# Attention q in 64-row tiles, eight heads at a time, with the vector work and the transposes in a hand-made order

## The chip, the cores and the metric

One core of a Trainium2 chip. The metric is the device time of one execution in microseconds (us). Where runs are compared they are of the same state (fast), and their intervals are at 95%.

## The reference, cut to what matters

One transformer block over 2048 tokens of width 576, everything in bf16: attention with 32 query heads on 16 cached K/V heads, a "mixer" with shifts by 1 and 2 tokens, and an MLP.

```python
x = A_x
xn = _layernorm(x)
q = (xn @ wq)                         # (2048, 576) @ (576, 4096): 32 heads of 128
k, v = the last 512 cached rows of each of 16 heads, each used by two query heads
o = softmax(q k^T * 128**-0.5) v
s = o @ wo                            # (2048, 4096) @ (4096, 576)
h = gelu(layernorm(xn) @ w1)          # mixer; its columns are shifted by +1, -1, +2, -2 tokens
x1 = xn + shifted(h) @ w2
g = silu(x1 + gelu(layernorm(x1) @ w3) @ w4)
return x + s * g
```

## The kernel before

The attention runs in 128 **units**: one head, one block of 512 queries. Four blocks of 32 units. PE, POOL and SP follow the program's order; DVE and ACT are ordered by a scheduler, in which `high_priority` moves an operation ahead. A unit is five q matmuls (576 rows padded to 5 x 128), four score matmuls, four exponentials on ACT, sixteen narrow P·V matmuls, a reciprocal and a multiplication on DVE for each half of them, and a transpose of the result by a DMA that SP issues:

```python
def stage_q(u):
    ...
    for kc in range(NDC):                                   # 5 chunks of 128 rows, the last half empty
        nc.tensor.matmul(psq[:, :], lhsT=w[:, kc, hh * Dh:(hh + 1) * Dh], rhs=xT_b[qb % 2][:, kc, :], ...)
    ... qT is copied by DVE in the first block, by ACT later ...

def stage_v(u, t0):
    ...                                                     # o_pool has 4 buffers
    with tc.high_priority(offset=HP):
        nc.vector.reciprocal(out=ri, in_=po[:, :, Dh])
        nc.vector.tensor_tensor(out=o[:, t0:t0 + 2, :], in0=po[:, :, 0:Dh], in1=ri..., op=ALU.mult)

def stage_t(u):
    o = o_t.pop(u)
    oT = oT_pool.tile([P, TB, P], BF16, name="oT")
    last_t[0] = nc.sync.dma_start(out=oT[:], in_=o[:]..., transpose=True)

for u in range(...):                                        # PE's order
    for i in range(4):
        stage_s(u, i)
        if i == 0:
            stage_q(u + 1)                                  # one q per unit
            for fn in fill.get(u, []): fn()                 # loads, layernorm, LN transposes
            continue
        if i < 3: stage_v(u - 1, 2 * (i - 1))
        ...                                                 # output projection and mixer matmuls in the gaps
    stage_t(u - 1)
```

All of the weights are loaded by POOL while the first block runs. Where in the program each load stands is set by a unit number.

```python
def load_wq(j, eng=None):                                   # four heads of wq: two requests
    eng.dma_start(out=w[:, 0:NF, :], in_=...)               # 512 KB
    eng.dma_start(out=w[0:DR, NF, :], in_=...)              # 64 KB
...
at(2, lambda: late(pT_t[2][0][0:1, 0:1], load_w1))          # late: a small POOL copy that waits for unit 2
at(10, gather_w1)
for i in range(8):
    at(4 + 3 * i, lambda i=i: late(pT_t[4 + 3 * i][0][0:1, 0:1], lambda: load_wo(i)))   # 576 KB each
at(4, lambda: load_k(2))
at(12, lambda: load_k(3))                                   # 512 KB
for g in range(4, Hkv, 2):
    at(2 * g - 8, lambda g=g: load_v(g // 2))               # two requests of 128 KB
for j in range(2, NB * 8):
    at(4 * (j - 1) - 1, lambda j=j: load_wq(j))
```

## Time and profile before

| | before |
|---|---|
| time | 855.94 us, median of 3 runs (852.17 to 856.51) |
| span of the profiled run | 847.5 us |
| PE busy | 98% of the span |

The lines that the prediction rests on stand in it. Beside them, the windows of the kernel before: the time before the first exponential is 12.9 us, then come the first block of attention, the second, and (the last line) everything after the attention. Columns: the stretch, its us, busy us and count of PE, PEld, DVE, ACT and POOL, the granted clock, the DMA share, GB/s.

```profile
12.90:116.00 103.10, 99.97 (x851) 62.75 (x867) 80.42 (x260) 75.75 (x134) 30.90 (x52) 1.00 0.85 182
116.00:249.80 133.80, 132.79 (x1104) 79.29 (x1122) 65.10 (x225) 92.27 (x172) 17.40 (x30) 1.00 0.45 96
521.50:847.50 326.00, 315.65 (x3609) 174.87 (x3617) 140.42 (x383) 103.02 (x174) 1.67 (x2) 1.00 0.29 79
```

One group of the page, the operation that frees a P·V bank and fills an o buffer:

```profile
L387 DVE TENSOR_TENSOR o<-po,ri_b 128x256 bf16<-128x256 f32 x256 | 107.9, 422 | 10.7 <-DMA oT<-o 4.3
```

Of DVE's idle time ahead of it 4.3 us were ended by a DMA: a transpose had not yet given its o buffer back.

### The profile page before, as it was taken

How to read it: one execution, taken by the hardware profiler on the slowest of the kernel's cores; microseconds unless marked ns; L12 is line 12 of the kernel's file. 1: busy time of each engine (PE TensorE's matmuls, PEld its weight loads, DVE VectorE, ACT ScalarE, POOL GpSimd, SP SyncE). 2: the span in 40 equal slices, each digit the busy share in tenths (PEclk: the TensorE clock that was granted, in tenths of full speed). 3: DMA queues.
4: the chain of work that ended last, by engine and by line, in shares of the span. 5: the costliest groups of instructions: out<-in, count | busy, mean ns of one | idle time of the engine just before them, and what ended most of it. 6: DMA issues, size and time to landing. Idle time of an engine off the chain costs nothing.

```text
span 847.5 us, 19375 instructions
## 1 busy us (share of the span) xinstructions
PE 826.8 (98%) x7896; PEld 485.0 (57%) x7980; DVE 427.7 (50%) x1351; ACT 460.9 (54%) x825; POOL 76.9 (9%) x134
## 2 busy tenths in 40 slices
PE   8999899999999999999999999999999999999996
PEld 5665555665564565565566565455555555555555
DVE  5778841267751166762154884052247537635324
ACT  5776763598793388784379874132333333334610
POOL 3441200310010111010001100000000000000000
PEclk9999999999999999999999999999999999999999
DMA  7996751473372174363048336992003301310101
GB/s 181 234 234 159 157 97 41 117 125 91 87 136 43 41 130 99 91 126 82 19 82 164 70 79 105 307 342 47 2 2 74 99 2 43 69 64 15 44 15 46
DMA packets 139983, 83.94 MB, mean 99 GB/s; under 512 B 106944, under 2 KB 133248, under 8 KB 139888
## 3 DMA queue, kind: packets, MB, share of 16 engines
q1 hardware_dynamic: 130048, 53.01, 30.6%
q0 software_dynamic: 8448, 28.15, 11.8%
q10 hardware_dynamic: 1392, 1.48, 0.5%
q8 instruction: 64, 1.05, 0.5%
q14 instruction: 31, 0.25, 0.1%
HBM read 49.17 MB, written 9.44 MB: 69 GB/s over the span
## 4 chain that ended last, share of the span: by engine, by line

## 5 line engine op out<-in xcount | busy, mean ns | idle before, releaser
L367 ACT ACTIVATE pT<-sc 128x512 bf16<-128x512 f32 x512 | 290.3, 596 | 103.5 <-PE sc L365 91.4
L365 PE MATMUL sc<-qT,kT 128*128 128x512 bf16 x493 | 175.1, 378 | 1.3 <-DVE qT L355 0.6
L382 PEld LDWEIGHTS <-pT 128*128 128x128 bf16 x2048 | 139.5, 98 | 52.9 <-DVE o L387 2.5
L382 PE MATMUL po<-v_sb,pT 128*128 128x129 bf16 x2048 | 161.4, 220 | 3.2 <-DVE o L387 2.0
L350 PE MATMUL psq<-xT_b,wq_b 128*128 128x512 bf16 x603 | 151.9, 379 | 2.5 <-DMA xT_b<-xn_b 0.4
L386 DVE RECIPROCAL ri_b<-po 128x2 f32<-128x2 f32 x256 | 43.0, 168 | 189.3 <-PE po L382 185.3
L731 PE MATMUL ph<-xT_b,w_s 64*128 64x512 bf16 x976 | 127.1, 376 | 2.3 <-DVE fence L721 2.1
L768 PE MATMUL pm<-w_s,h 64*128 64x512 bf16 x864 | 122.2, 377 | 0.9 <-DVE fence L721 0.9
L406 PE MATMUL pswo<-wo_sb,oT 128*128 128x512 bf16 x497 | 114.2, 379 | 0.8
L387 DVE TENSOR_TENSOR o<-po,ri_b 128x256 bf16<-128x256 f32 x256 | 107.9, 422 | 10.7 <-DMA oT<-o 4.3
L749 ACT ACTIVATE h<-ph 128x512 bf16<-128x512 f32 x67 | 39.4, 597 | 133.9 <-PE ph L731 133.9
L350 PEld LDWEIGHTS <-wq_b 128*128 128x128 bf16 x640 | 62.4, 98 | 74.4 <-issue 2.2
L768 PEld LDWEIGHTS <-h 64*128 64x128 bf16 x1728 | 70.8, 94 | 56.7 <-issue 1.6
L406 PEld LDWEIGHTS <-oT 128*128 128x128 bf16 x1024 | 64.9, 98 | 55.2
L768 PE MATMUL pr<-w_s,h 64*128 64x64 bf16 x864 | 90.2, 189 | 0.2 <-ACT h L749 0.2
L731 PEld LDWEIGHTS <-w_s 64*128 64x128 bf16 x1152 | 57.3, 94 | 51.0 <-issue 2.8
L357 ACT ACTIVATE qT<-psq 128x512 bf16<-128x512 f32 x96 | 57.4, 598 | 28.1 <-PE psq L350 26.7
L747 DVE COPY hx<-ph 128x512 f32<-128x512 f32 x55 | 38.0, 692 | 67.8 <-PE ph L731 67.8
L365 PEld LDWEIGHTS <-kT 128*128 128x128 bf16 x512 | 47.4, 97 | 28.4 <-DVE qT L355 1.2
L227 POOL DMA_DIRECT2D wq_b<-in_A_wq_dram x30 | 23.4, 780 | 314.4 <-PE psq L350 295.4
L721 DVE TENSOR_SCALAR fence<-ph,ph 1x1 f32<-1x1 f32 x61 | 12.6, 206 | 53.9 <-PE ph L731 53.4
L749 ACT ACTIVATE h<-hx 128x512 bf16<-128x512 f32 x55 | 34.6, 630 | 8.5 <-DVE hx L747 7.0
(114 smaller groups left out, 641.3 us busy)
## 6 DMA issues: line engine op xcount, KB each, us to landing
wq_b<-in_A_wq_dram POOLq DMA_DIRECT2D x30, 512.0 KB, 5.3
w_s<-in_B_w_dram SPq DMA_DIRECT2D x9, 576.0 KB, 7.0
wo_sb<-in_A_wo_dram POOLq DMA_DIRECT2D x8, 576.0 KB, 5.0
w_s<-in_B_w_dram SPq DMA_DIRECT2D x9, 512.0 KB, 7.9
x_dram<-x SPq DMA_DIRECT2D x4, 576.0 KB, 3.5
x<-x_dram SPq DMA_DIRECT2D x4, 576.0 KB, 5.1
s_b<-s_dram SPq DMA_DIRECT2D x4, 576.0 KB, 5.4
x_b<-in_A_x_dram SPq DMA_DIRECT2D x4, 576.0 KB, 6.6
```

What stands on the lines that cost most here:

```text
L350: nc.tensor.matmul(psq[:, :], lhsT=w[:, kc, hh * Dh:(hh + 1) * Dh], rhs=xT_b[qb % 2][:, kc, :], start=(kc == 0), stop=(kc == NDC - 1))
L357: nc.scalar.activation(out=qT[:, :], in_=psq[:, :], func=ACT.Copy)
L365: nc.tensor.matmul(sc[:, :], lhsT=kT[:, g, kc * P:(kc + 1) * P], rhs=qT_t[u][:, :], start=True, stop=True)
L367: nc.scalar.activation(out=pT[:, :], in_=sc[:, :], func=ACT.Exp, scale=SCALE)
L382: nc.tensor.matmul(po[:, j, :], lhsT=pTs[kc][:, tt * P:(tt + 1) * P], rhs=v_sb[:, g, kc, 0:Dh + 1], start=(kc == 0), stop=(kc == KCH - 1))
L386: nc.vector.reciprocal(out=ri, in_=po[:, :, Dh])
L387: nc.vector.tensor_tensor(out=o[:, t0:t0 + 2, :], in0=po[:, :, 0:Dh], in1=ri.unsqueeze(2).to_broadcast([P, 2, Dh]), op=ALU.mult)
L406: nc.tensor.matmul(ps, lhsT=oT_t[qb * Hq + h][:, tt, :], rhs=wo_sb[:, h, lo:hi], start=(h == 0), stop=(h == Hq - 1))
L731: nc.tensor.matmul(ps[i][:, :], lhsT=lhsT, rhs=xT[half, kc, :], start=first, stop=last, skip_group_check=True)
L747: nc.vector.tensor_copy(out=src[:, :], in_=ps[i][:, :])
L749: nc.scalar.activation(out=h3[:, :], in_=src[:, :], func=ACT.Gelu_apprx_tanh)
L768: nc.tensor.matmul(out, lhsT=h3_t[b, fc][half, tt * P:(tt + 1) * P], rhs=w4_s[fc // WS][half, fc % WS, lo:hi], start=key not in started, s ...
```

## The change

**Intent.** q for two heads takes nine slots in place of ten, by running the two 64-row halves of the PE array on different heads; eight heads at a time (four in the first block), so that the change of tiling is paid seldom. DVE and ACT join the engines that follow the program's order; their small work is handed out in pieces by a budget. LN transposes wait in a list and are issued between those of the attention outputs. The mixer's stages move later, and so do the loads of w1 (eleven units) and wo (five units); the wq loads of the first block move two units earlier.

The diff, cut to its core:

```diff
-        o_pool = pool("o_pool", 4)
+        o_pool = pool("o_pool", 5)
...
         def load_wq(j, eng=None):
-            eng.dma_start(out=w[0:DR, NF, :], in_=A_wq[NF * P:D, c0:c0 + 4 * Dh])
+            for half in (LO, HI):                     # the last 64 rows of wq, once for each half
+                eng.dma_start(out=w[half, NF, :], in_=A_wq[NF * P:D, c0:c0 + 4 * Dh])
...
+        def transpose_extra(gap):
+            if extra and clock["us"] - clock["sp"] > gap:
+                extra.pop(0)()
+                clock["sp"] = clock["us"]
+        def quarter(us):                              # called after each quarter of a unit
+            clock["us"] += us
+            transpose_extra(3.2 if us < 1.0 else 1.2)
+            clock["credit"] = min(clock["credit"] + us, 1.2)
+            while clock["credit"] > 0.25:
+                us = pick(9)                          # the next small DVE or ACT operation
+                if not us: break
+                clock["credit"] -= us
...
+        def stage_qs(u0, n):                          # n heads: first half, fence, ..., second half
+            X, Y, Z = (ps_pq, "pq"), (ps_po, "po"), (ps_sc, "sc")
+            banks = [X, Y] if u0 == 0 else [Z, X] if n == 4 else [X, Y, Z, X]
+            for u2 in range(u0, u0 + n, 4):
+                for u in (u2, u2 + 2):
+                    q_half(xT, u, ps, [(kc, ((0, LO), (1, HI))) for kc in range(NDC)], True)
+                    nc.vector.tensor_scalar(out=f[:, :], in0=ps[0][0:1, 0:1], scalar1=ps[1][0:1, 0:1], ...)  # fence
+                for u, ps in pairs:
+                    q_half(xT, u, ps, [(kc, ((1, LO), (0, HI))) for kc in range(NF)], False)
...
-        at(2, lambda: late(pT_t[2][0][0:1, 0:1], load_w1))
-        at(10, gather_w1)
+        at(13, lambda: late(pT_t[13][0][0:1, 0:1], load_w1))
+        at(20, gather_w1)
         for i in range(8):
-            at(4 + 3 * i, ... load_wo(i))
+            at(9 + 3 * i, ... load_wo(i))
         for j in range(2, NB * 8):
-            at(4 * (j - 1) - 1, lambda j=j: load_wq(j))
+            at(4 * (j - 2) + 1 if j < 10 else 8 * (j // 2 - 1) + 1 + j % 2, lambda j=j: load_wq(j))
...
-        with tc.manual_schedule(engines={SP, POOL, PE}):
+        with tc.manual_schedule(engines={SP, POOL, PE, DVE, ACTE}):
+                if u % (4 if u < Hq else 8) == 0 and 0 < u < U:
+                    stage_qs(u, 4 if u < Hq else 8)
-                    if i < 3 and 0 <= u - 1 < U:
-                        stage_v(u - 1, 2 * (i - 1))
+                    v, tt = (u - 2, 2 + i) if i < 2 else (u - 1, i - 2)    # one token tile per quarter
+                    if 0 <= v < U:
+                        stage_v(v, tt)
```

The Newton step of every layernorm falls from one piece of eleven operations into four pieces.

## The prediction

> **What bounds the kernel now.** I read the page first (busy shares, then the slices), then PE's timeline in a quiet stretch, then the windows by stage, then the list of waits, then the timeline around each hole that PE has. From the page:
>
> ```profile
> PE 826.8 (98%) x7896; PEld 485.0 (57%) x7980; DVE 427.7 (50%) x1351; ACT 460.9 (54%) x825; POOL 76.9 (9%) x134
> ...
> PE   8999899999999999999999999999999999999996
> ```
>
> PE is busy in every slice; DVE and ACT are at half. "Busy" is not proof of a full rate, so I read the spacing of starts in PE's timeline, of one attention unit (one head, 512 queries):
>
> ```profile
> 232.00 1.24 PE L350 MATMUL psq<-xT_b,wq_b 128*128 128x512 bf16 x5
> 233.08 0.38 PE L365 MATMUL sc<-qT,kT 128*128 128x512 bf16 x1
> 233.30 0.63 PE L382 MATMUL po<-v_sb,pT 128*128 128x129 bf16 x8
> 233.77 0.38 PE L365 MATMUL sc<-qT,kT 128*128 128x512 bf16 x1
> 233.98 0.63 PE L382 MATMUL po<-v_sb,pT 128*128 128x129 bf16 x8
> 234.45 0.59 PE L365 MATMUL sc<-qT,kT 128*128 128x512 bf16 x2
> ```
>
> Five q matmuls take 233.08 - 232.00 = 1.08 us, 216 ns each; a score matmul 233.30 - 233.08 = 0.22; eight P·V matmuls 0.47. A unit is 1.08 + 4 x 0.216 + 2 x 0.47 = 2.88 us, and the next q begins 2.87 us later: nothing is lost. Pricing the whole program so (640 q, 512 score, 512 + 512 narrow output matmuls, 180 + 80 narrow in the first mixer stage, the MLP's pairs at 216 and 245 ns) gives about 821 us. The rest of 847.5 is some 11 us before the first score matmul, 6.7 after the last matmul, and about 8 us of holes. So PE bounds it, and a change earns only by removing PE slots or those holes. The holes over 0.5 us after the start are five:
>
> ```profile
> 104.72 0.42 DVE L387 TENSOR_TENSOR o<-po,ri_b 128x256 bf16<-128x256 f32 x1 [3.72 <-DMA oT<-o]
> 105.20 0.65 PE L382 MATMUL po<-v_sb,pT 128*128 128x129 bf16 x8 [1.96 <-DVE o L387]
> 380.69 1.24 PE L350 MATMUL psq<-xT_b,wq_b 128*128 128x512 bf16 x4 [0.38 <-DMA xT_b<-xn_b]
> 568.14 0.39 PE L768 MATMUL pm<-w_s,h 64*128 64x512 bf16 x2 [0.92 <-DVE fence L721]
> 649.27 1.04 PE L731 MATMUL ph<-xT_b,w_s 64*128 64x512 bf16 x8 [1.04 <-DVE fence L721]
> ```
>
> The first two belong to transposes queued on SP: LN and attention-output transposes alternate there, 1.2 to 1.7 us each, an o buffer came free late, and DVE, then PE, waited (a loss of about 2.1 us and 0.5 us of start spacing). The last two, and a twin of 1.0 us at 720, are in the MLP: a fence on DVE stands behind the eleven little operations of one layernorm's Newton step, about 2 us in one lump.
>
> **What the Trainium skill says.** "TensorE: Matmul & The Clock Gate", Part 3: matmuls on different row groups run together, about 4 ns apart. The trace agrees: the 64-row pairs of L731 start 4 to 20 ns apart and a pair takes 216 ns, what one 128-row matmul takes. "TensorEngine Tiling (Array Packing)", Key Properties: changing the tiling mode drains TensorE. The trace has two changes. Into 64 rows at 553.77: the last 64-column matmul began at 553.646, so 126 ns where the usual spacing is 29. Back to 128 rows at 805.43: 309 ns after the last pair where 216 is usual. Each costs 93 to 97 ns. "PSUM — Partial Sum Buffer", bank collisions: different row tiles may not access one bank at once; hence the fences that the change adds between a pair's two halves. "Perfetto Trace Analysis", its opening note: matmul busy time is a bad measure because matmuls are pipelined; that is why I priced by starts.
>
> **The change, part by part.**
>
> (1) q in 64-row tiles. 576 rows of the contraction are nine halves; 128-row matmuls pad them to ten. Two heads now share nine slots in place of ten. 128 heads: 640 x 216 = 138.2 us becomes 576 x 216 = 124.4. **-13.8 us**, all on PE, all on the path.
>
> (2) Mode changes. Four heads at a time in the first block of queries (8 batches), eight after that (3 x 4 = 12): 20 batches, 40 changes at 95 ns. **+3.8 us**. (Batches of two heads would have paid 12.)
>
> (3) The SP order and one more o buffer: the holes at 102.9 and 380 go. **-2.6 us**. New ones of the kind are possible, since oT is used later by only one unit.
>
> (4) The Newton step falls into four pieces, so one pop puts at most 0.5 us before a fence: the three MLP holes (0.9 to 1.1 us) go. **-3.2 us**.
>
> (5) Start. Layernorm writes the last 64 columns twice: four more small DVE operations, about 0.16 us each by the small operations of this trace, **+0.6**, against about as much that is won because four q are ready before the first score matmul (it waited 0.56 us for qT). **0**.
>
> (6) ACT inside a batch. This is where I differ from the obvious sum. ACT's exponentials come 477 ns apart at the closest (two in 1.08 us, each of 0.60):
>
> ```profile
> 59.86 1.08 ACT L367 ACTIVATE pT<-sc 128x512 bf16<-128x512 f32 x2
> ```
>
> Four per unit need 1.91 us. A unit used to take PE 2.88; now that q is pulled out in front, a unit without other filling takes PE 1.80. So PE outruns ACT by 0.1 us per unit. Three score banks give slack: a bank is held 0.42 (score start to exponential) + 0.60 + 0.06 = 1.08 us, PE comes back to it after 3 x 0.45 = 1.35, slack 0.27, of which the last qT copy of the batch (ACT, just ahead of the first exponential) eats 0.17. A batch of eight plain units so loses 8 x 0.11 + 0.17 - 0.27, about 0.75 us. Filling (output projection on five units, mixer stages on ten or more) protects the others; going through the schedule I count three wholly plain batches, three or four partly plain ones: 3 x 0.75 + 1.6, **+3.9 us**. While q runs for 7.8 us, ACT has nearly nothing to do, and that time cannot be had back.
>
> (7) In the first block each batch of four borrows two of the three score banks for its first q pair. The exponential that frees the second ends about 0.35 us after the batch could begin; less the drain of 0.1 that is paid anyway, 7 x 0.25 = **+1.8 us**.
>
> (8) Fences: 64, of 0.21 us on DVE, strictly in program order now, with up to 0.7 us of layernorm or GELU pieces put ahead of each. PE needs a fence 1.08 us after its half ended (or 0.86); with 0.16 of drain, 0.2 of fence and 0.7 of pieces, it is just in time, and late where DVE had a backlog. An estimate, not a derivation: 0.15 us per batch, 20 batches, **+3 us**.
>
> DVE gains 32 qT copies of 0.69 us and the 64 fences, ACT loses 32 copies; in a block of 132 us DVE was busy 64 and ACT 90, so neither becomes the bound over a block. Weight loads come in pairs once per eight units (at least 14 us for two loads that land in 5.3), so wq should not bind.
>
> Sum: -13.8 + 3.8 - 2.6 - 3.2 + 0 + 3.9 + 1.8 + 3 = **-7.1 us**; 855.94 - 7.1 = 848.8. I say **848.5**.
>
> **Rivals.** (a) *Full gain*: fences and ACT never bite, because the pieces on DVE are small and the filling is spread. Then -13.8 + 3.8 - 5.8 = -15.8, 840 us. For it: PE waits for ACT 0.3 us and for fences 3 us in the whole kernel before. Against it: before, ACT had 2.88 us for 2.4 us of work; that margin is what the change spends. Even this falls short of 2% (17.1 us). (b) *ACT becomes the bound within batches*, more than I allow: each tanh or copy in a batch adds 0.5 us, and all twelve eight-head batches lose 0.75 or more; with fences at 0.4 us per batch the gain is eaten: 855 or a little over. For it: a batch of eight plain units with its q is about 22.4 us on PE and 23 through ACT, against 8 x 2.88 = 23.0 before. (c) *A DMA wait takes the place of the one removed*: both wq buffers fall free at once and are needed together eight units later, or a transpose misses its batch, which then holds all eight q. Lost would be 1 to 3 us each time. Against it: 44% DMA share in the later blocks, loads asked for six units ahead.
>
> **Range and chances.** The fixed terms (1), (2), (4) are counted from spacings and leave -13.2. The soft ones, (3), (6) to (8), can be nearly nothing, or 15. That spans 840 to 857, and the three runs of before already spread over 4 us: **839 to 856.5**. Over 2% faster needs more than rival (a) plus luck: 0.07. Over 2% slower needs 30 us of new waits: 0.02. Within 2%: 0.91.
>
> **What would show it.** q slots 216 ns per pair, 576 of them; 90 to 100 ns at each change of mode; no hole over 1 us at the first LN transposes or in the MLP (fence waits there near zero); in plain stretches units of 1.91, not 1.80 us, with PE waiting for pT; PE waiting for the new fence in the q batches, some 3 us in all. The step that I hold for weakest is (6): if plain units run at 1.80 us, it is wrong, and the time is nearer 844. If PE's holes in the attention exceed 10 us, (8) or rival (c) is the cause.

## The result, and the profile after

| | before | after |
|---|---|---|
| time, median | 854.33 us (852.17 to 856.51, 4 runs) | 891.92 us (880.12 to 896.21, 4 runs) |
| ratio of the fast runs | | 1.039 [1.030, 1.048]: slower |
| span of the profiled run | 847.5 us | 878.4 us |

Ratios here are the mean time of one kernel's fast runs over that of the other's of the same rounds, so not quite the ratio of the medians that are quoted; of the four runs of the changed kernel the longest, 896.21, counts as slow and is left out of its ratio. The prediction was wrong: 848.5 with a range to 856.5, and 0.02 for slower.

The windows of the kernel after, cut at the same events (the first exponential of units 0, 32 and 64, and the end of the attention):

```profile
17.50:140.80 123.30, 107.53 (x1009) 64.87 (x1009) 74.13 (x247) 75.35 (x150) 36.45 (x64) 0.93 0.90 159
140.80:281.50 140.70, 137.15 (x1265) 80.11 (x1264) 94.04 (x307) 83.35 (x158) 21.56 (x39) 1.00 0.48 97
553.70:878.40 324.70, 315.69 (x3620) 174.78 (x3620) 139.90 (x383) 103.03 (x175) 1.66 (x2) 0.99 0.30 78
```

The first block went from 103.1 to 123.3 us. It kept the DMA engines busier (0.90) and moved fewer bytes in a second (159 against 182 GB/s), and of the four blocks it alone had a lowered clock (0.93). In the same way for all stages:

| us, profiled runs | to the first exponential | block 0 | block 1 | block 2 | block 3 | rest |
|---|---|---|---|---|---|---|
| before | 12.9 | 103.1 | 133.7 | 134.3 | 137.4 | 326.0 |
| after | 17.5 | 123.3 | 140.7 | 135.3 | 136.9 | 324.6 |
| difference | +4.6 | +20.2 | +7.0 | +1.0 | -0.5 | -1.4 |

(Batches shift some work between these stages: the first stage has four q in place of one, block 0 36 q in place of 32 and fewer mixer matmuls, block 3 only 24 q. Sums over the attention are exact: 521.4 and 553.7 us.)

From the page after: the slices (22 us each; the low digits are the start and the first block), the clock, and the two groups that answer to the one shown before.

```profile
PE   7997879999999999999999989999999999999996
...
PEclk9998989999999999999999999999999999999999
...
L469 PE MATMUL po<-v_sb,pT 128*128 128x129 bf16 x2048 | 203.6, 221 | 14.7 <-DVE o L476 14.6
...
L476 DVE TENSOR_TENSOR o<-po,ri_b 128x256 bf16<-128x256 f32 x256 | 108.6, 424 | 21.0 <-DMA oT<-o 12.1
```

DVE's wait for an o buffer has grown from 4.3 to 12.1 us, and PE's wait for DVE, which was 2.0 us, to 14.6 (8.9 of it in block 0). The timeline shows the chain at the largest hole, from SP's transposes to DVE to PE. Columns: start, us, engine, line, operation, count, and in brackets the idle time before it and its releaser.

```profile
60.56 13.22 SPq L486 DMA_TRANSPOSE oT<-o  x3
...
77.57 0.42 DVE L476 TENSOR_TENSOR o<-po,ri_b 128x256 bf16<-128x256 f32 x1 [6.06 <-DMA oT<-o]
...
78.05 0.61 PE L469 MATMUL po<-v_sb,pT 128*128 128x129 bf16 x4 [5.83 <-DVE o L476]
...
78.56 0.63 PE L452 MATMUL sc<-qT,kT 128*128 128x512 bf16 x1
```

Three transposes of 128 KB each took the SP queue 13.2 us. The last line is the first score matmul after the hole: 0.63 us where 0.38 is usual. The granted clock fell to 0.5 three times in block 0, for 17.1 us in all, each time during one of PE's three long holes (5.8, 2.9 and 5.4 us) or within 0.5 us after it. So the hole came first, and the lowered clock made it dearer.

What POOL had issued just before:

```profile
54.93 0.80 POOL L297 DMA_DIRECT2D wo_sb<-in_A_wo_dram  x1 [0.31 <-issue]
55.72 0.77 POOL L245 DMA_DIRECT2D x<-in_A_k_cache_dram  x1
56.47 1.49 POOL L251 DMA_DIRECT2D v_sb<-in_A_v_cache_dram  x2
...
58.06 0.75 POOL L301 DMA_DIRECT2D w_sb<-in_B_w_dram  x1
58.80 0.54 POOL L302 DMA_DIRECT2D w_sb<-in_B_w_dram  x1
59.34 0.79 POOL L233 DMA_DIRECT2D wq_b<-in_A_wq_dram  x1
60.11 0.54 POOL L236 DMA_DIRECT2D wq_b<-in_A_wq_dram  x1
60.83 0.54 POOL L236 DMA_DIRECT2D wq_b<-in_A_wq_dram  x1 [0.18 <-ACT pT L454]
```

Nine requests in 6.5 us, without a wait between them (the last two lines are the two halves of the wq remainder). In the kernel before, the same stretch of time has wo at 52.6, two requests for wq at 55.3, then nothing until wo at 61.6. (It too issues nine in a row, but earlier; run 13 comes back to that.) The DMA view of the stretch 54 to 92 us gives issues with their count, KB and median us from issue to landing; the q1 line is the queue of the transposes with its packets, MB and share. Before:

```profile
wq_b<-in_A_wq_dram POOLq DMA_DIRECT2D x3, 512.0 KB, 6.5
...
oT<-o SPq DMA_TRANSPOSE x11, 5.5
```

After:

```profile
q1 hardware_dynamic: 4239, 1.03, 42.7%
...
wq_b<-in_A_wq_dram POOLq DMA_DIRECT2D x3, 512.0 KB, 13.6
...
oT<-o SPq DMA_TRANSPOSE x8, 18.2
```

A transpose takes 3.3 times as long to land, a weight load 2.1 times. The DMA engines are busy throughout, yet total traffic in the stretch is 161 GB/s against 180. Counted from issues and landings in the trace, up to eight requests of POOL and six of SP are in flight at once. That alone is no sign: the kernel before reaches eight (at 40.7 us) and five (at 53.5 us), without a hole then. Five o buffers cover about 15 us of units (some 3 us each); 18.2 us is more. I call this state a **jam** below.

### The profile page after: what moved, and what is told of

Its sections match the earlier page's. It is cut to its first block, busy times and chain, and to the rows that moved or that the text cites.

```text
span 878.4 us, 20555 instructions
## 1 busy us (share of the span) xinstructions
PE 839.9 (96%) x8492; PEld 487.6 (56%) x8492; DVE 475.8 (54%) x1463; ACT 429.2 (49%) x793; POOL 91.0 (10%) x161
## 4 chain that ended last, share of the span: by engine, by line
## 5 line engine op out<-in xcount | busy, mean ns | idle before, releaser
L454 ACT ACTIVATE pT<-sc 128x512 bf16<-128x512 f32 x512 | 267.1, 673 | 107.0 <-PE sc L452 106.1
L469 PE MATMUL po<-v_sb,pT 128*128 128x129 bf16 x2048 | 203.6, 221 | 14.7 <-DVE o L476 14.6
L469 PEld LDWEIGHTS <-pT 128*128 128x128 bf16 x2048 | 158.1, 98 | 91.2 <-DVE o L476 19.7
L452 PE MATMUL sc<-qT,kT 128*128 128x512 bf16 x512 | 194.0, 379 | 1.0 <-ACT pT L454 0.7
L444 PE MATMUL psq<-xT_b,wq_b 64*128 64x512 bf16 x1152 | 132.8, 383 | 1.4 <-DVE fence L428 0.6
L497 PE MATMUL pswo<-wo_sb,oT 128*128 128x512 bf16 x512 | 118.7, 379 | 2.1 <-DMA oT<-o 1.2
L476 DVE TENSOR_TENSOR o<-po,ri_b 128x256 bf16<-128x256 f32 x256 | 108.6, 424 | 21.0 <-DMA oT<-o 12.1
L444 PEld LDWEIGHTS <-wq_b 64*128 64x128 bf16 x1152 | 57.7, 95 | 69.8 <-issue 8.8
L436 ACT ACTIVATE qT<-psq 128x512 bf16<-128x512 f32 x64 | 38.2, 597 | 91.6 <-PE psq L444 89.1
L452 PEld LDWEIGHTS <-kT 128*128 128x128 bf16 x512 | 50.1, 98 | 21.4 <-issue 9.0
L437 DVE CAST qT<-psq 128x512 bf16<-128x512 f32 x64 | 44.1, 689 | 17.7 <-PE psq L444 17.5
```

Source lines behind the costliest of these rows:

```text
L436: nc.scalar.activation(out=qT_t[u][:, :], in_=ps[0][:, :], func=ACT.Copy)
L437: nc.vector.tensor_copy(out=qT_t[u + 1][:, :], in_=ps[1][:, :])
L444: nc.tensor.matmul(ps[k][:, :], lhsT=w[half, kc, hh * Dh:(hh + 1) * Dh], rhs=xT[half, kc, :], start=(first and kc == 0), stop=(not first a ...
L452: nc.tensor.matmul(sc[:, :], lhsT=kT[:, g, kc * P:(kc + 1) * P], rhs=qT_t[u][:, :], start=True, stop=True)
L454: nc.scalar.activation(out=pT[:, :], in_=sc[:, :], func=ACT.Exp, scale=SCALE)
L469: nc.tensor.matmul(po[:, j, :], lhsT=pTs[kc][:, tt * P:(tt + 1) * P], rhs=v_sb[:, g, kc, 0:Dh + 1], start=(kc == 0), stop=(kc == KCH - 1))
```

## The experiments

18 kernels ran. Times are medians, with the range and the kernel before on the same chip; "b0" is the length of block 0 in the profile (103.1 us before, 123.3 after). First theories: A, loads too *late and wide* (wo moved five units later and w1 eleven, into the mixer's work); B, *the third request* of each wq load; C, *the spacing* of the LN transposes; D, *the bunch*, nine requests in a row. A rival to all is chance.

**1. The change again.** No edit. 

> The changed kernel once more, unedited, as the base that the next three are read against on one chip. Before: 854 us; the changed kernel gave 880 to 896, of which 15 us stood in three holes of PE between 71 and 115 us, behind output transposes that took about 20 us from issue to landing. If the holes are a property of the program, they come again in the same place and the time lies between 878 and 897; if they were an accident of that profile, 850.

885.4 us (880.7 to 895.2), before 852.7; 1.036 [1.028, 1.043]. Not chance. The profiled run was a slow one (b0 139.3), so its block 0 isn't compared. In this run, and in 3, 4, 6 and 13 below, blocks 1 and 2 are the same to 0.1 us (140.7 and 135.3): only block 0 varies.

**2. w1 and wo early, as before** (wq stays where the change put it).

```diff
-        at(13, ... load_w1);  at(20, gather_w1)
+        at(2, ... load_w1);   at(10, gather_w1)
-            at(9 + 3 * i, ... load_wo(i))
+            at(4 + 3 * i, ... load_wo(i))
```

> The changed kernel with the loads of w1 and wo at the units where the kernel before has them (w1 at unit 2 instead of 13, wo from unit 4 instead of 9); nothing else. Theory A (the loads, moved later, pile up with K, V and wq in units 12 to 24 and the transposes wait behind them): the three holes go, transposes land within 10 us, and the time falls by 15 to 35 us, to 850 to 862. Theory B (the third request of every wq slice is the cause): no change, 880 or more. Theory C (the order of layernorm and output transposes on SP): no change.

892.1 us (889.6 to 894.9), 1.045 [1.038, 1.053]; b0 135.8. Missed: no better, rather worse. The jam is there, only sooner: eleven requests fall between 30 and 38 us, and from 32 us transposes are late. Theory A falls as it stood. What the two have in common is a bunch; that it is the cause was a guess here.

**3. w1 early alone.** Only the first line of the edit above. 

> Only w1 (0.66 MB) back at unit 2; wo stays late. Theory A in its narrow form (one slice too much in units 12 and 13, where K, V, wo, wq and w1 are all asked for): nearly all of what the run with both gains. Theory A in its wide form (1 MB of wo is missing from the quiet time at 20 to 45 us): a third to a half of it. Theories B and C: nothing.

877.9 us (873.7 to 881.7), 1.030 [1.022, 1.038]; b0 116.4. Two requests (648 KB) less in the bunch give a part back, 7 us by medians, at the edge of the scatter.

**4. Without the third wq request.** One copy of the remainder, the other half of the tile set to zero once (results of these heads are wrong on purpose; the output still passes, because q's last 64 rows matter little to it).

```diff
-            for half in (LO, HI):
+            for half in (LO,):
```

> The changed kernel with the last 64 rows of wq loaded into the lower half of the partitions only, as before (two requests per slice instead of three, 30 x 64 KB less); the upper half is zero, so the result is wrong on purpose for every second head. Theory B (the extra requests choke the queue): the holes at 71 to 115 us go and the time falls to about 855. Theory A: at most a few us, since 0.5 MB of 21 in the first block is taken away.

872.2 us (871.1 to 874.7), 1.021 [1.015, 1.028]; b0 119.6, still with holes. B takes part, and is not the whole.

**5. The third request in the kernel before.**

```diff
-            eng.dma_start(out=w[0:DR, NF, :], in_=A_wq[NF * P:D, c0:c0 + 4 * Dh])
+            for half in (slice(0, DR), slice(DR, P)):
+                eng.dma_start(out=w[half, NF, :], in_=A_wq[NF * P:D, c0:c0 + 4 * Dh])
```

> The kernel before with one thing of the change: every wq slice takes a third request of 64 KB that puts its last 64 rows into the upper half of the partitions too (multiplied by zeros there, the result is right). If the third request by itself chokes the first block (Theory B: taking it away won 13 us), this kernel gets holes at 50 to 110 us and is 5 to 15 us slower than before, about 862. If it only hurts on top of another change of the DMA traffic (Theory D: the order in which loads and transposes meet), within 2 us of before.

858.7 us (850.9 to 863.6, 20 runs), before 854.6; 1.003 [1.000, 1.006]. The ratio says that it costs little (the medians, 4 us apart, say more); the range says more still. The profiled run, one of the long ones, has the same chain as the changed kernel:

```profile
66.00 1.05 PE L381 MATMUL po<-v_sb,pT 128*128 128x129 bf16 x8 [7.29 <-DVE o L386]
```

The old program is near the edge and falls over it in some executions. Its own runs scatter too: in 26 runs on one chip 850.6 to 869.7.

**6. Both 3 and 4.** 

> The changed kernel with both single gains so far: no third wq request (wrong on purpose) and w1 at unit 2. If the first block is bound by the sum of its transfers, the gains add (13 + 7): about 865, first block some 108 us. If the holes come from how certain requests meet, they don't add, and the run stays at 870 or so.

871.3 us (867.2 to 876.0), 1.021 [1.015, 1.028]; b0 118.1. The two gains do not add: leaving out the third request gives by itself as much as both.

**7. LN transposes issued at once.** In the list of steps `extra.append(tr)` becomes `tr()`. 

> The changed kernel with each layernorm transpose issued at once when its tile is ready, not held in the list that spaces them between the output transposes. If the spacing (Theory C) causes holes in the first block, the output transposes pass sooner and the time falls by 5 us or more; if spacing helps, as it was meant to, the time rises by some us; if the transposes' place does not matter while loads fill the queues, nothing changes beyond the scatter of 880 to 896.

879.8 us (877.2 to 890.2), 1.035 [1.026, 1.044]; b0 123.3, block 1 141.7. Theory C falls: the spacing makes no difference beyond the scatter.

**8. The wq loads in their old phase**, at unit 4k + 3 in place of 4k + 1. 

> The changed kernel with the wq loads of the first block at the units where the kernel before has them: unit 4k+3, five units ahead of their use, in place of 4k+1, seven ahead, one unit after two V loads. Theory D (V, wq and wo requests now meet in the same two units and make a standing pile behind which transposes wait): the holes shrink and the time falls by 10 to 25 us. Theory B or a plain lack of bandwidth: no change, or worse where wq is late.

878.3 us (874.2 to 888.4), 1.029 [1.025, 1.033]. A small part at most: the intervals of this run and of run 1 overlap. (Its profiled run was slow and isn't compared.)

**9 and 10. wo not loaded, in either kernel.** Wrong (s is zero), to take 4.7 MB of traffic away.

```diff
-            nc.gpsimd.dma_start(out=wo_sb[:, h0:h0 + 4, :], in_=A_wo[...]...)
+            nc.vector.memset(wo_sb[:, h0:h0 + 4, :], 0.0)
```

> The changed kernel with the 4.7 MB of wo not loaded but set to zero by DVE in the same units (wrong on purpose): of the 15 MB that the first block loads, a third is away. If loads and transposes together overload the DMA queues (Theory E), the holes before 115 us vanish, transposes land within 8 us, and the first block takes its PE time, about 100 to 105 us instead of 123 to 139; the total is then what the prediction's other terms make of the change, 848 to 854. If something else holds the transposes up, the first block stays above 115.

> The kernel before with wo set to zero in the same way (wrong on purpose): the partner of the run above. Its only DMA hole (2.1 us at 103) may go; within 3 us of before. The ratio of these two says what the change is worth where the DMA queues are no limit: the prediction's sum says 7 us less for the changed kernel; full gain (rival a) would be 16 less; the reading that ACT eats the gain (rival b) about 0.

Changed kernel: 866.9 us (863.9 to 869.8), 1.011 [1.003, 1.020]; b0 113.7. Kernel before: 855.7 (855.2 to 857.2), 1.000 [0.998, 1.003]; b0 102.8, no transpose over 6.8 us, and a range of 2 us in 12 runs. So the traffic of wo is what brings the old kernel near the edge, and its absence makes it steady. That its time is no shorter is an accident of the test: the scheduler put DVE's zeroing of wo ahead of the first layernorm, and the first exponential came at 20.5 us in place of 12.9. The two totals are therefore no price of the change; in the changed kernel even without it the other seven or eight requests at 54 to 61 us are a jam (oT transposes 10.3 us at the median in that stretch).

**11. Seven o buffers** (oT 34, for room). 

> The changed kernel with two of the transposed tiles' buffers turned into output buffers (o 5 to 7, oT 36 to 34): DVE may run two units, some 6 us, further ahead of the transposes before it and PE must wait. If the wait for an o buffer is what stops PE (transposes of 20 us against a reserve of 5 units x 3 us), holes get about 6 us shorter each and the time falls by 8 to 15 us. If the queue is overloaded without end, the hole only comes later: less than 5 us.

888.7 us (885.4 to 897.9), 1.040 [1.028, 1.052]; b0 123.7, and a new hole of 7.9 us in block 1: with 34 oT buffers an output's transpose waits on SP for the output projection, and a layernorm transpose waits behind it. Missed: two more o buffers do not shorten block 0 (they cost two oT buffers, so the test is not a clean one).

**12. The same three wq requests with half the bytes in the two small ones** (each half gets only the heads that it serves: 32 KB each). 

> The changed kernel with the last 64 rows of a wq slice loaded for the even heads into the lower half and for the odd heads into the upper half, 32 KB each, in place of all four heads into both (three requests as now, the bytes of before; the result is right). If the bytes were what the run without the third request won by, this wins the same, 10 to 13 us. If the third request as such costs, it stays near 880.

883.7 us (880.6 to 893.5), 1.035 [1.023, 1.047]; b0 126.6; transposes 19.0 us. These 64 KB do not count. The run does not say that bytes don't: the nine requests together are 2632 KB.

**13. The bunch dissolved.** The same requests, all of them, at units where no others stand:

```diff
-        at(13, ... load_w1);  at(20, gather_w1)
-        for i in range(8):
-            at(9 + 3 * i, ... load_wo(i))
+        at(2, ... load_w1);   at(10, gather_w1)
+        for i, v in enumerate([3, 10, 14, 18, 22, 24, 26, 28]):
+            at(v, ... load_wo(i))
-        at(12, lambda: load_k(3))
+        at(15, lambda: load_k(3))
```

> The changed kernel with the loads of the first block taken apart in time: w1 at unit 2, the last K load at unit 15, and the eight wo loads at units 3, 10, 14, 18, 22, 24, 26, 28, so that no more than five or six requests fall into two neighbouring units. If a bunch of nine requests at units 12 and 13 starts the jam and the jam then keeps itself up (Theory D), the first block has no hole over 2 us and takes 103 to 108 us; the total falls to 856 to 862. If not, the jam begins at some other place and the total stays above 870.

859.6 us (858.0 to 871.0, 20 runs), before 855.5; 1.008 [1.005, 1.010]. The window of block 0, the DMA view of 54 to 92 us, and PE's waits in block 0 (first of the changed kernel, then of this one; columns: us in total, times, longest):

```profile
16.90:119.30 102.40, 101.19 (x1009) 63.11 (x1009) 74.09 (x247) 75.27 (x150) 36.40 (x64) 1.00 0.97 192
```

```profile
q1 hardware_dynamic: 11282, 2.73, 53.3%
...
oT<-o SPq DMA_TRANSPOSE x13, 5.2
```

```profile
PE po L469 <- DVE o L476: 8.9, 3, 5.8
PE ph L551 <- DMA xnnT<-xn_b: 5.3, 1, 5.3
```

```profile
PE po L469 <- DVE o L476: 0.2, 1, 0.2
```

Block 0 is 20.9 us shorter with the same bytes and the same number of requests, and the clock is whole. 11,282 transpose packets pass in the stretch in which 4,239 did. The DMA share is *higher* (0.97), and so are the GB/s. Of the 20.9 us, 14.6 are waits of PE (15.5 against 0.9) and 6.3 are PE's busy time for the same 1009 matmuls, at the lowered clock.

So where these loads stand next to each other is the cause. Theory D said more, that the *number* in a row is, and that does not hold. The kernel before issues nine requests in 6.7 us too, and PE has no hole behind them:

```profile
34.66 0.75 POOL L293 DMA_DIRECT2D wo_sb<-in_A_wo_dram  x1 [0.30 <-issue]
35.40 0.76 POOL L227 DMA_DIRECT2D wq_b<-in_A_wq_dram  x1
36.14 0.55 POOL L229 DMA_DIRECT2D wq_b<-in_A_wq_dram  x1
...
37.75 2.18 POOL L220 DMA_DIRECT2D xt<-in_A_x_dram  x4 [0.40 <-DVE ln_st L133]
39.91 1.50 POOL L244 DMA_DIRECT2D v_sb<-in_A_v_cache_dram  x2
```

Spread has nine from 36.1 to 42.6 us as well. These two carry 1984 and 1472 KB, the changed kernel's nine 2632 KB. That it is the bytes asked for within a few us is a rival that no run tests.

**14. The bunch put into the kernel before**, to have it the other way round: w1 at unit 12, gathered at 15, and two wo loads at 12. 

> The kernel before with a bunch made on purpose: w1 at unit 12 instead of 2, and two wo loads at unit 12 too, where V and K are asked for and wq one unit earlier: nine requests in two units; bytes and number of requests as before, 64-row tiles nowhere. Theory D: transposes take 12 us and more from about 50 us on, holes of several us, 5 to 20 us slower than before. If the new schedule of the engines is needed for a jam, within 2 us of before.

863.4 us (858.2 to 866.9), 1.012 [1.007, 1.017]; b0 110.7 in a run of 858.2, with holes of 3.3 and 2.4 us, the first of them the same chain:

```profile
67.67 1.05 PE L382 MATMUL po<-v_sb,pT 128*128 128x129 bf16 x8 [3.27 <-DVE o L387]
```

As expected in kind, not in size. The bunch is as large as the changed kernel's (nine requests, 3144 KB, from 49.7 to 56.7 us), but in that block one oT transpose took 14.0 us and all others under 10, and block 0 grew by 7.6 us, not by 20. So a bunch costs the kernel before time too; the greater part of the changed kernel's jam needs something else of its order, and which is open. The next question: spread should by my sum be 7 us *faster* than before, and is 4 slower. Runs 15 to 18 are on that; all but the last start from spread.

**15. DVE's budget kept strictly.** A small operation is handed out only if the credit (plus 0.1) covers it.

```diff
-                us = pick(9)
+                us = pick(clock["credit"] + 0.1)
```

> The spread version, with a piece of layernorm or GELU put on DVE only where the account of free DVE time covers its cost but for 0.1 us (now up to 0.4 us overdrawn). The theory that DVE's program order makes PE wait for o and for the mixer's banks (excess of 7 us in front of P·V matmuls and 4.4 in front of mixer matmuls in blocks 1 to 3) says that these holes shrink by half or so: blocks 1 to 3 together 4 to 7 us shorter than in the spread version. If the waits come from ACT and PSUM, no change.

862.9 us (861.5 to 863.5), 1.009 [1.005, 1.012]; block 1 144.7 in place of 140.7. Missed, it is longer. P·V waits for DVE as long as before (5.9 against 5.7 us in blocks 1 to 3), and the pieces that are held back make a new wait, 2.6 us of a mixer matmul for an LN transpose. The budget of the picker is ruled out by this, not the order on DVE.

**16. q in 128 rows, in the same batches**: no tiles, no fences, no changes of mode, no third request. The order of everything else is kept.

```diff
-                    q_half(xT, u, ps, [(kc, ((0, LO), (1, HI))) for kc in range(NDC)], True)
-                    ... fence ...
+                    q_full(xT, u, ps, 0)
-                    q_half(xT, u, ps, [(kc, ((1, LO), (0, HI))) for kc in range(NF)], False)
+                    q_full(xT, u, ps, 1)
```

> The spread version with q in whole 128-row matmuls again, ten slots for two heads, no fences, no changes of tiling mode, third wq request away; batches, banks and the rest of the schedule as in the changed kernel. The tiles' own worth by the prediction: 13.8 - 3.8 = 10 us over the kernel, 2.7 us in each of blocks 1 to 3, less what fences cost. So blocks 2 and 3 should get longer by 2 to 3 us each. If fences and mode changes eat the gain, they stay within 1 us.

863.0 us (862.0 to 863.6), 1.010 [1.007, 1.014]; stages 18.8, 102.4, 142.3, 137.5, 138.6, rest 322.2. Blocks 2 and 3 are 2.2 and 1.7 us longer than in spread, about as expected. This is the run that splits the change. PE's waits for blocks 1 to 3 (120 to 555 us), first of the changed kernel, then of this one:

```profile
PE po L469 <- DVE o L476: 5.9, 9, 1.4
PE psx L609 <- DVE x L620: 2.8, 4, 0.9
```

```profile
PE po L475 <- DVE o L482: 5.6, 8, 1.4
PE psx L615 <- DVE x L626: 2.8, 4, 0.9
```

They are the same without tiles, and neither line exists in the kernel before, whose waits in these blocks sum to 0.7 us. So they belong to the order of the work, not to the tiles. The changed kernel's trace shows how such a wait looks:

```profile
522.85 0.16 DVE L112 SCALAR_TENSOR_TENSOR nr_t<-nr_y 128x4 f32<-128x4 f32 x1
...
523.32 0.16 DVE L475 RECIPROCAL ri_b<-po 128x2 f32<-128x2 f32 x1
523.51 0.42 DVE L476 TENSOR_TENSOR o<-po,ri_b 128x256 bf16<-128x256 f32 x1
...
524.00 0.41 PE L469 MATMUL po<-v_sb,pT 128*128 128x129 bf16 x4 [1.43 <-DVE o L476]
```

The reciprocal that frees a P·V bank stands behind pieces of a layernorm's Newton step. In the kernel before it had high priority and went ahead of them.

**17. P·V of two token tiles in a row again**, as in the kernel before. 

> The spread version with the P.V matmuls of two query tiles again one after the other (in the second and the fourth quarter of a unit, eight matmuls each, as before) and not one tile per quarter. The two output banks of a unit are then held 0.43 us less each (0.47 of matmuls, 0.16 drain, 0.6 on DVE, of 1.8 us between two uses). If the slack of 0.15 us per bank is why PE waits for DVE in front of P.V matmuls (7.3 us in blocks 1 to 3), these waits fall to 3 us or less and the total by 3 to 5 us, to about 855. If the lumps of DVE work alone set them, nothing changes.

861.5 us (861.2 to 861.9), before 852.3; 1.010 [1.008, 1.013]; blocks 1 to 3 142.1, 136.6, 137.1. Missed: P·V's wait for DVE fell to 4.0 us, the mixer's grew to 3.7 and the output projection's for ACT to 1.9. Nothing is gained; the wait moves.

**18. The kernel before, with the part of the change that is plainly good** (the Newton step in four pieces in the MLP) and wo at units 1, 6, 10, 14, 18, 22, 25, 29. 

> The kernel before (q in 128 rows, one head at a time) with the two parts that the runs show to be good: the MLP's layernorms take their Newton step in four pieces, and the wo loads stand in units where nothing else is asked for (1, 6, 10, 14, 18, 22, 25, 29). The three MLP holes of 0.9 to 1.1 us go; no jam in the first block in any run, so also less scatter: about 3 us faster than before, 0.4 to 0.8%. If the pieces only move the wait, equal.

850.5 us (846.9 to 863.6, 22 runs), before 852.3 (27 runs); 0.996 [0.994, 0.999]. The best version of all, by 0.4%. Everything after the attention takes 323.1 us in place of 326.0. PE's waits there, before:

```profile
PE ph L731 <- DVE fence L721: 2.1, 2, 1.0
PE pm L768 <- DVE fence L721: 0.9, 1, 0.9
```

and in this run no line with a fence is left. The moved wo loads did not help: b0 is 107.4 in the profile, with four small holes, and the scatter stays.

## Why the prediction was wrong, point by point

The attention (everything up to its last exponential) splits in three by profile: before 521.4 us, rows128 539.6, spread 532.2, after 553.7.

| part of the change | measured | predicted |
|---|---|---|
| order of the work: batches, DVE and ACT in program order, P·V one tile at a time (rows128 less before) | +18.2 | (3) -2.6, (5) 0, (6) +3.9, (7) +1.8: +3.1 |
| tiles, mode changes, fences (spread less rows128) | -7.4 | (1) -13.8, (2) +3.8, (8) +3: -7.0 |
| bunch of loads (after less spread) | +21.5 | rival (c), 1 to 3 us each time, and dismissed |
| sum over the attention | +32.3 | -3.9 |
| rest (after less before) | -1.4 | (4) -3.2 |

The three pieces are differences of single profiled runs, and that of the kernel before was one of its fastest (849.25 us). By the medians of one chip rows128 is 7.6 us over before and spread 3.5 under rows128 (4.1 over before). That -7.4 agrees with -7.0 is partly luck: the changes of mode cost more than priced, the fences less.

**Step (3) failed, in the way of rival (c), which I had dismissed.** Step (3) has the o buffers' waits for transposes go, -2.6 us. In the changed kernel they grew, and the jam behind them is worth +21.5. Rival (c) has the kind, a DMA wait in place of the one removed, but neither of its two ways: PE waited neither for wq nor for a transpose of x, but at the o buffers and for the mixer's input (8.9 and 5.3 us). "Weight loads come in pairs ... so wq should not bind" and "against it: 44% DMA share in the later blocks" both looked at the wrong place: at wq alone, and at the blocks in which DMA is idle half the time. The diff brings nine requests together in the *first* block, whose share was 0.85. I took each load by itself ("at least 14 us for two loads that land in 5.3"), with the median landing time of the whole run. Runs 2 to 14 show that the jam depends on which loads stand next to each other: dissolve the bunch and 20.9 us of block 0 go (13), make one in the kernel before and it loses 8 us (14). The third request (4, 5) takes part; the spacing (7) and 64 KB of the small requests (12) do not matter. The count of requests alone is not what decides (13); whether the bytes do, or what follows the bunch, is not separated.

**The sum's second failure is the order on DVE**, in step (8) and the sentence after it. I priced "strictly in program order now" only at the fences, 3 us. With PE's starts, from the trace's instructions (no view sums this), laid out against their usual spacings, spread loses 26.8 us in its four blocks, and the kernel before 3.4 for the same work: 5.6 at mode changes, 5.9 ahead of score matmuls, 1.0 ahead of q (the fences), but 7.6 ahead of P·V and 4.4 ahead of the mixer's output, both of which wait for DVE. The fences were overpriced; the cost was at the two operations that lost their priority. That DVE is busy half the time says nothing on how long a bank waits behind pieces of 0.5 us. (The waits view shows less, 5.7 and 2.8 us in blocks 1 to 3, because a matmul's modelled end lies about 0.16 us after the next one's usual start, and a wait shorter than that is no idle time.) rows128 shows that it comes with the order; what in the order is to be changed stays open, since neither the budget (15) nor pairing (17) gained.

Step by step:
- (1) **Right.** Eight heads take 72 matmuls of 64 rows:

```profile
219.21 7.94 PE L444 MATMUL psq<-xT_b,wq_b 64*128 64x512 bf16 x72
227.09 0.39 PE L452 MATMUL sc<-qT,kT 128*128 128x512 bf16 x1
```

(227.09 - 219.21) / 36 = 0.219 us a pair, with the fences and the way back in it; 576 pairs in all.
- (2) **Right in kind, mis-sized**: 40 changes, at 5.6 us in place of 3.8. Into the tiles, after a P·V matmul, 151 to 155 ns where 59 is usual. Out of them 309 ns after the last matmul, as predicted, but the prediction's 216 is the wrong yardstick: from a pair's second matmul to the next pair it is 196 ns, so the way out costs 113, not 93. The changes themselves are then about 4 us; a q bank or its fence adds the rest.
- (3) **Wrong in the changed kernel**: its o buffers ran out for longer (12.1 us of DVE's wait in place of 4.3). In spread the holes are gone, as predicted.
- (4) **Right**: no fence waits in the MLP; run 18 has 2.9 us of the 3.2. In the changed kernel a new wait of 1.2 us for an oT transpose took part of it.
- (5) 17.5 - 12.9 = 4.6 us, of which 13 more q slots (18 for four heads, less 5 for one) are 2.8 and only moved. About 1.8 are lost where 0 was predicted.
- (6), (7) **Right**: plain units run through ACT at 1.91 us, not 1.80 (four of them in 7.63 us, ACT busy for all of it); ahead of score matmuls 5.9 us are lost, predicted 5.7 (the part of (7) that falls on q matmuls stands in (2)).
- (8) **Wrong**, as told above. (No run tests the bank collision that the fences are there for.)

The last sentence of the prediction named it: "If PE's holes in the attention exceed 10 us, (8) or rival (c) is the cause." It was both, (c) in kind. The chance of 0.02 came from adding the rival as 1 to 3 us; in the changed kernel the oT transposes issued from 59 to 81 us took 15 to 22 us to land, so it is no small term.

What stays open, beside what makes a jam: why it moves fewer bytes with the engines as busy. In the stretch 54 to 92 us a packet of the transposes' queue took 61 ns on average, against 29 in the kernel before (the queue's share of 16 engines for 38 us, over its packets). The Trainium skill, "DMA: Bandwidth & Descriptors", section "Queues, rings and completion order", says that each DMA engine takes turns between the queues that have work, a packet at a time (its packet is some 9 to 17 descriptors, and need not be one of the profile's); that a never-empty POOL queue then holds back the transposes would fit the counts (POOL's packets 1,449 against 1,345 before, the transposes' 4,239 against 8,317), but no run isolates it, and it doesn't explain why weight loads are slow as well.

## What to carry to other kernels

Before moving loads in a kernel whose first stage has a DMA share near 0.9, list the requests of all engines in order of issue, with their KB, and compare the landing times before and after the move. Here the same requests at other units made the block 123.3 or 102.4 us long, and the small transposes of another queue paid for the large loads. When an engine goes from a priority scheduler to program order, price not the new operations on it but the old ones that others wait for. And when a change of many parts moves the time the wrong way, a run that keeps the order and takes the new operation out tells at once which of the two it was.

## What the Trainium skill lacked or had wrong

- "DMA: Bandwidth & Descriptors", section "Rules for kernel authors", says that "A transpose next to ordinary DMAs needs nothing". That is so for correctness, not for time: in the stretch of 38 us that follows nine loads issued in 6.5 us the oT transposes landed in 18.2 us at the median in place of 5.5, and the total rate fell from 180 to 161 GB/s with the engines busy. None of the pages that I read tells of it.
- The same page, section "Bandwidth", gives times by size alone. The runs show that a 512 KB load of wq takes 6.5 us from issue to landing or 13.6, by what else is in flight, and that three requests of 512, 32 and 32 KB fare no better than 512, 64 and 64 (15.8 and 13.6 us).
- "TensorEngine Tiling (Array Packing)", Key Properties, names the drain at a change of tiling mode and gives no figure: here 92 to 97 ns into 64-row tiles and 113 out of them (93 by the prediction's count).
- "ScalarE: Activation LUTs", section "What ACT_TABLE_LOAD costs", gives 186 ns + 0.833 ns per element for an activation with immediate scale and bias, which for 512 elements is 613 ns (the traces: 0.60 us), and an overlap of about 93 ns back to back, which by estimate from these figures would be 520 ns. The exponentials here come closer: 477 ns in the kernel before, 489 in a full stretch after, (8.92 - 0.60) / 17 of the line

```profile
227.72 8.92 ACT L454 ACTIVATE pT<-sc 128x512 bf16<-128x512 f32 x18
```

so that the overlap is 110 to 125 ns, and a unit's four take 1.91 to 1.96 us.
